# Pooling four batches of keys and values with accumulating transfers instead of VectorE reductions, and a new order for all engines

## The chip, the cores and the metric

The kernel runs on one core of a Trainium2 chip. The metric is the device time of one execution in microseconds, the median of several runs. Before the change it is 791.49 us (three runs, 791.37 to 791.86).

## The reference

Attention of 8 batches with 8 heads of 64 on 576 tokens, with keys and values averaged over groups of 8 neighbours (72 keys are left), and behind it a normalisation, a two-layer network (512 to 2048 to 512, relu) and a residual:

```python
k_p = k.reshape(B, H, Sp, pool, D).mean(axis=3)        # pool = 8, Sp = 72
v_p = v.reshape(B, H, Sp, pool, D).mean(axis=3)
scores = scale * np.matmul(q, k_p.transpose(0, 1, 3, 2))
attn = softmax(scores); attn_out = np.matmul(attn, v_p)
x = attn_out.transpose(0, 2, 1, 3).reshape(B, S, H * D)
xn = (x - mu) / np.sqrt(var + 1e-06) * g_ln
return x + np.maximum(xn @ w_ch1, 0.0) @ w_ch2
```

All is float32. The kernel makes each float32 factor from a high and a low float16 part and a product from three matmuls.

## The kernel before, in words

The 4608 tokens are 36 tiles of 128, four tiles to a chunk of 512 columns, nine chunks. Each tile goes through `stage_a` (load q, scores, softmax numerators; the maximum `mx` at L800, the difference `e` at L805), `probs_turned`, and `stage_b`, that is `values` (its product with the pooled values is scaled to the tile `x` at L950 on VectorE, then measured for the normalisation) and `parts_turned` (transposes of x on TensorE, L881). Chunks 0 and 1 take the network directly (`ffn_in` with matmuls at L1116 and results in `ring` at L1125 on ScalarE and L1127 on VectorE, `ffn_out` with sums at L1330); later chunks take a seven-product scheme (`product` at L1160, `out_seven` at L1277, sums at L1294). Its factors are made between them: ScalarE casts (L1196), VectorE and GpSimd subtract (L1198, L1215 to L1219); `sums_w2` makes sums of w2 with temporaries in the tile `kr` (L1239 on VectorE, L1244 to L1252 on GpSimd). At the start `convert` rebuilds the weights (L527 to L543), and `split_w` cuts them into parts, the high one on ScalarE (L483), the low one on VectorE (L490).

Keys and values must be pooled for each batch before its tiles. `half_k` and `half_v` do half a batch each: a load on SP's queue per pair of heads (288 KB into `kr`, L645) or per head (144 KB into `vr`, L659), and a reduction over 8 values: on VectorE with one `tensor_reduce` (L655 into `kblk`, L666 into `vp`), or for batch 2's keys and batch 1's and 2's values on GpSimd with three additions.

Nothing is ordered by a scheduler. Each stage is a generator, and two lists of tokens, `START` and `STEADY`, say which generator goes on by one step next ("HV.4.0" is the next step of half_v(4, 0)). So every engine's queue stands in the order of the lists, and an engine waits at its next instruction even where a later one could run. `kr` and `vr` have two buffers each, and `kr` is shared with `sums_w2`.

Of the kernel before, what the change touches and what calls it, by code (L numbers as in the profile page):

```python
# [63 lines left out]
START = """
LN.2 Q.0 LK.0 LN.2 LK.1 R.1.0 Q.1 A.0 R.1.1 R.1.2 K0 V0 K0 A.0 R.1.3 A.0 A.0 K0 R.1.3 R.1.2 HV.1.0 LK.0 LK.1 LG V0 R.2.0
E.0.0 LG V0 C.1.0 C.1.0 C.1.0 C.1.0 R.2.0 E.0.0 E.0.0 V0 V0 E.0.1 A.1 A.1 V0 A.1 E.1.0 C.1.1 V0 Q.1 C.1.1 E.0.1 C.1.1
C.1.1 E.0.0 V0 V0 C.1.2 C.1.3 E.0.1 C.1.2 E.1.0 E.0.1 E.1.1 HV.1.0 E.1.1 HV.1.0 E.1.1 C.1.3 E.1.1 E.1.0 HV.1.0 E.1.0
R.2.1 HV.1.0 HK.1.0 R.2.1 A.2 A.2 M1.0 A.2 A.2 B.0 A.1 M1.0 M1.0 M1.0 S.1.0 E.2.0 B.0 S.1.0 C.2.0 S.1.1 C.1.2 R.1.1 B.0
E.2.1 Q.0 HV.1.0 S.1.0 A.3 E.2.1 E.2.0 A.3 A.3 C.1.3 S.1.1 HK.1.0 E.2.1 A.3 E.2.0 E.2.1 B.0 B.0 B.0 B.0 S.1.2 E.2.0
R.1.0 B.1 HK.1.0 R.2.2 E.3.0 B.1 R.2.2 E.3.1 E.3.0 E.3.1 E.3.0 E.3.1 B.1 B.1 B.1 B.1 B.1 C.1.3 E.3.1 E.3.0 HV.1.0 C.2.0  # L70
HK.1.0 C.1.2 S.1.2 B.2 B.2 HV.1.1 C.2.2 S.1.3 HV.1.1 C.2.1 B.2 HV.1.0 B.2 B.2 C.2.0 B.2 B.2 S.1.3 HK.1.0 C.2.0 S.1.3 B.3
HK.1.1 HK.1.1 S.1.2 HK.1.1 C.2.1 HK.1.1 HK.1.1 C.2.1 C.2.1 B.3 F.0.0.0 F.0.1.0 F.0.0.0 F.0.1.0 F.0.0.0 R.2.3 D.0 R.2.3
F.0.1.0 A.4 F.0.0.0 F.0.2.0 A.4 F.0.1.0 F.0.3.0 A.4 HV.1.0 HV.1.1 C.2.2 HV.1.1 B.3 C.2.3 F.0.2.0 F.0.3.0 F.0.2.0 A.4
F.0.2.0 A.4 F.0.3.0 F.0.3.0 C.2.3 D.0 F.0.4.0 R.1.4 HV.1.1 A.5 A.5 A.5 C.2.2 C.2.2 HV.1.1 HV.1.1 C.2.3 F.0.4.0 B.3 B.3
B.3 B.3 R.1.4 F.0.5.0 A.5 F.0.6.0 R.1.5 M2.0 M2.0 F.0.5.0 F.0.4.0 F.0.6.0 F.0.4.0 A.5 M2.0 M2.0 R.1.6 S.1.1 A.6 S.2.0
A.6 R.1.7 C.1.4 R.1.7 F.0.5.0 A.4 R.1.5 A.4 HV.1.1 F.0.5.0 F.0.6.0 A.6 S.2.0 F.0.7.0 F.0.0.1 HV.1.1 F.0.0.1 F.0.1.1
HV.1.1 HV.1.1 F.0.1.1 F.0.7.0 HV.1.1 F.0.7.0 HV.1.1 HV.1.1 D.1 D.1 S.2.1 F.0.1.1 C.1.4 F.0.0.1 S.2.1 C.1.7 F.0.2.1 S.2.0
A.7 A.7 R.1.6 C.1.5 F.0.3.1 F.0.3.1 F.0.3.1 C.2.3 F.0.2.1 S.2.2 S.2.2 S.2.2 F.0.2.1 F.0.3.1 HV.1.1 F.0.4.1 F.0.2.1
F.0.5.1 C.1.6 M1.1 F.0.4.1 F.0.5.1 F.0.4.1 F.0.5.1 F.0.5.1 C.1.4 A.6 F.0.4.1 F.0.6.1 B.4 A.5 S.2.3 M1.1 B.4 M1.1 F.0.7.0
A.6 C.1.5 S.2.3 F.0.7.1 F.0.7.1 F.0.7.1 F.0.7.1 G.0.0.0 B.4 F.0.0.1 F.0.1.1 F.0.6.1 S.2.3 C.1.4 A.7 F.0.6.1 C.1.5 A.6  # L80
A.6 S.1.4 G.0.0.0 R.2.4 R.2.4 R.2.5 R.2.5 A.7 C.1.7 B.5 B.4 G.0.1.0 F.0.6.1 A.7 A.7 A.7 B.4 G.0.2.0 C.1.6 C.1.7 C.1.6
S.1.4 R.2.6 R.2.7 S.1.5 B.5 B.5 S.1.5 G.0.1.0 R.2.6 R.2.7 G.0.2.0 G.0.2.0 HK.2.0 G.0.3.0 C.2.4 S.1.6 C.2.5 S.1.6 B.6 B.4
C.2.4 G.0.1.0 B.4 S.1.7 G.0.3.0 S.1.7 F.0.8 HV.2.0 G.0.3.0 B.5 C.2.4 B.5 B.5 F.0.8 B.6 F.0.8 F.0.9 C.2.5 B.5 C.2.6
F.0.10 A.5 C.2.7 C.2.6 F.0.8 F.0.9 F.0.9 F.0.6.0 F.0.11 C.2.5 C.2.7 C.2.5 C.2.6 C.2.7 C.2.7 HK.2.0 F.0.10 C.2.6 F.0.11
B.6 C.2.4 C.1.5 M2.1 S.1.4 F.0.9 HK.2.0 F.0.12 M1.1 HK.2.1 F.0.10 A.8 HK.2.1 HK.2.0 HV.2.0 F.0.10 S.1.7 M2.1 M2.1 S.2.4
S.1.5 F.0.11 HV.2.0 F.0.12 S.2.4 F.0.12 A.8 S.2.5 F.0.12 F.0.13 S.2.4 F.0.11 S.2.5 S.2.5 HK.2.0 HV.2.0 HV.2.0 F.0.13 B.6
F.0.14 HV.2.0 C.1.7 HK.2.1 B.7 HV.2.0 G.0.0.0 S.2.6 F.0.14 HK.2.1 F.0.15 B.6 HK.2.1 F.0.13 F.0.13 S.2.6 S.2.7 S.2.7
F.0.14 F.0.14 F.0.15 S.2.7 HV.2.0 F.0.15 C.1.6 B.7 A.8 B.7 F.0.15 HV.2.0 B.7 A.8 HK.3.0 G.0.0.1 HV.2.1 HK.3.0 HV.2.1 B.7
A.8 HV.2.1 HV.2.1 HV.2.1 B.6 A.8 A.9 G.0.1.1 G.0.2.1 S.1.6 HV.2.1 B.6 B.7 HV.2.1 HV.3.0 G.0.0.1 G.0.1.1 A.9 G.0.2.1 B.7
A.8 A.9 A.9 G.0.3.1 A.9 T.1.0 HV.2.1 A.10 A.10 A.11 A.9 G.0.3.1 T.1.0 G.0.3.1 G.0.3.1 HV.2.1 F.1.0 A.9 B.8 T.1.0 T.1.0  # L90
F.1.0 HK.3.0 A.10 G.0.1.1 G.0.1.1 F.1.1 T.1.0 A.11 B.8 T.1.0 F.1.0 HV.2.1 S.2.6 T.1.0 S.2.1 T.1.0 F.1.2 F.1.0 T.1.0 A.10
T.1.0 HV.2.1 F.1.1 T.1.0 T.1.0 HV.2.1 F.1.1 F.1.2 F.1.2 F.1.3 HV.2.1 F.1.4 F.1.2 F.1.5 HV.2.1 HV.3.0 HV.3.0 T.1.1 HV.2.1
HV.2.1 G.0.2.1 F.1.1 F.1.4 F.1.4 G.0.2.1 HV.3.0 F.1.4 F.1.3 HV.3.0 A.10 A.11 A.10 HV.3.0 F.1.3 T.1.1 A.11 HV.3.0 F.1.3
F.1.6 B.9 F.1.6 T.1.1 F.1.5 HV.3.0 HV.3.0 A.10 T.1.1 A.11 HV.3.1 F.1.5 T.1.1 G.0.0.1 F.1.7 T.1.1 A.11 G.0.0.1 F.1.6
F.1.5 HV.3.1 T.1.1 A.11 HV.3.1 T.1.1 F.1.7 F.1.7 G.1.0.0 G.1.0.0 G.1.0.0 B.9 HV.3.1 G.1.1.0 HV.3.1 F.1.6 T.1.1 HV.3.1
G.1.2.0 HV.3.1 T.1.1 T.1.1 M2.1 HK.3.1 T.1.1 T.0.0 T.0.0 T.0.0 T.0.0 HV.3.1 T.0.0 T.0.0 V.10 G.1.3.0 T.0.0 T.0.0 HK.3.0
HK.3.0 T.0.0 T.0.0 F.1.7 T.0.0 G.1.2.0 HV.3.1 T.0.0 F.1.8 T.0.1 G.1.1.0 F.1.9 T.0.1 F.1.8 T.0.1 G.1.3.0 G.1.3.0 T.0.1
V.10 B.8 B.8 T.0.1 T.0.1 T.0.1 T.0.1 F.1.10 HV.3.1 F.1.8 HV.3.1 F.1.8 HV.3.1 T.0.1 F.1.9 U.0.1 U.0.0 F.1.11 F.1.10
F.1.11 F.1.9 T.0.1 F.1.9 B.8 F.1.10 B.11 B.8 F.1.10 U.0.1 G.1.1.0 F.1.12 B.11 U.0.1 T.0.1 F.1.13 F.1.12 T.0.1 F.1.13
F.1.11 F.1.11 F.1.14 F.1.12 F.1.14 F.1.13 F.1.13 B.9 F.1.15 F.1.15 B.9 U.1.1 B.9 U.1.0 F.1.14 F.1.14 F.1.15 F.1.15 B.9  # L100
B.9 V.10 V.10 HV.3.1 V.10 U.1.0 G.1.0.1 V.10 G.1.1.1 HV.3.1 F.1.12 U.1.0 HK.3.1 HK.3.1 V.10 V.10 G.1.2.1 G.1.0.1 X X
B.11 B.11 B.11 B.11 G.1.1.1 G.1.2.0 G.1.3.1 HV.3.1 HV.3.1 B.11 G.1.0.1 B.11 G.1.0.1 B.11 U.0.0 U.0.0 HK.3.1 HK.3.1 U.1.1
U.1.1 G.1.2.1 G.1.2.1 G.1.2.1 G.1.1.1 G.1.1.1 G.1.3.1 G.1.3.1 G.1.3.1
# [1358 lines left out]
```

## Time and profile before

| | |
|---|---|
| median of three runs | 791.49 us |
| the profiled execution | 792.71 us, of which the span of the trace is 791.0 us |
| TensorE (PE) busy | 772.5 us of the span (98%) |
| VectorE (DVE), GpSimd (POOL), ScalarE (ACT) busy | 628.3, 492.3, 469.5 us |
| mean granted TensorE clock | 1.00 of full speed |
| share of the 16 DMA engines in use by the main queue | 65.1% |

The profiled execution is one execution with the profiler on; 1.7 us of its time lie around the span. PE is the engine that is nearly always busy, so the end moves with what PE waits for. Busy time of the other engines costs nothing by itself; it counts where PE, or an engine that PE waits for, stands still for it.

### The profile page before, as it was taken

Reading aid. Unit: us, or ns where it says so; the run is one execution under the profiler, and the core shown is the slowest. Engines: PE = TensorE matmul, PEld = TensorE weight load, DVE = VectorE, ACT = ScalarE, POOL = GpSimd, SP = SyncE. Lnnn points to the kernel's source line nnn. Section 1 sums busy time; section 2 is a strip of 40 time slices with the busy share of each in tenths; the row PEclk is TensorE's granted clock in tenths of the full one; section 3 lists DMA queues with packets and bytes.
Section 4 is the critical chain, followed back from the end, with each engine's and each line's share of the span. In section 5 each row is a group of like instructions: output and inputs, shape, how many; then the busy total and the mean of one; then the engine's idle time right before and its main releaser. Section 6 shows DMA issues by size and latency. Waiting matters only on the chain. (4 is left out here: it accounts for less than half of the span.)

```text
span 791.0 us, 18982 instructions
## 1 busy us (share of the span) xinstructions
PE 772.5 (98%) x7458; PEld 592.8 (75%) x7458; DVE 628.3 (79%) x1296; ACT 469.5 (59%) x880; POOL 492.3 (62%) x597
## 2 busy tenths in 40 slices
...
GB/s 353 302 247 180 252 137 80 170 106 78 43 128 177 151 167 225 186 258 190 204 202 164 241 169 255 151 205 180 228 93 208 176 179 141 175 144 150 81 120 134
DMA packets 181513, 139.01 MB, mean 176 GB/s; under 512 B 143792, under 2 KB 151600, under 8 KB 179248
## 3 DMA queue, kind: packets, MB, share of 16 engines
q1 hardware_dynamic: 180272, 136.91, 65.1%
...
q10 hardware_dynamic: 1152, 0.90, 0.5%
...
## 5 line engine op out<-in xcount | busy, mean ns | idle before, releaser
L1277 PE MATMUL ps_f<-ring,w 128*128 128x256 f16 x2016 | 231.7, 273 | 1.5 <-DVE x L1294 1.0
L1277 PEld LDWEIGHTS <-w 128*128 128x128 f16 x2016 | 196.2, 98 | 25.8 <-issue 1.8
L1160 PE MATMUL ps_f<-zts,w 128*128 128x256 f16 x1680 | 208.1, 273 | 1.3 <-DVE x L1330 0.8
L1160 PEld LDWEIGHTS <-w 128*128 128x128 f16 x1680 | 162.7, 98 | 22.6 <-issue 2.1
L1319 PE MATMUL ps_f<-w,ring 128*128 128x512 f16 x576 | 126.6, 379 | 0.1
L1319 PEld LDWEIGHTS <-ring 128*128 128x128 f16 x576 | 56.0, 98 | 66.2 <-DVE ring L1127 0.9
L1179 ACT COPY raw<-ps_f 128x256 f32<-128x256 f32 x160 | 56.2, 372 | 81.7 <-PE ps_f L1160 69.3
L1160 PE MATMUL ps_f<-zts,tsp 128*128 128x256 f16 x672 | 92.1, 273 | 0.5 <-DVE raw L1174 0.3
L1116 PE MATMUL ps_f<-zts,w 128*128 128x512 f16 (+1 forms) x480 | 86.5, 336 | 2.9 <-DVE ring L1127 1.6
L1196 ACT CAST w<-w 128x512 f16<-128x512 f32 x96 | 59.0, 619 | 42.3 <-POOL w L1219 24.2
L1116 PEld LDWEIGHTS <-w 128*128 128x128 f16 x480 | 45.8, 98 | 38.8 <-issue 2.7
L1198 POOL TENSOR_TENSOR w<-w 128x512 f16<-128x512 f32 x48 | 57.4, 1197 | 25.5 <-ACT w L1196 22.9
L1160 PEld LDWEIGHTS <-tsp 128*128 128x128 f16 x672 | 64.5, 98 | 8.8 <-issue 0.7
L1215 POOL TENSOR_TENSOR w<-raw 128x256 f32<-128x256 f32 x32 | 25.9, 809 | 64.9 <-ACT raw L1207 42.9
L1294 DVE SCALAR_TENSOR_TENSOR x<-ps_f,y,x 128x256 f32<-128x256 f32 (+1 forms) x84 | 42.6, 518 | 28.5 <-PE ps_f L1277 27.5
L826 POOL TENSOR_TENSOR phl<-e,phl 128x512 f16<-128x512 f32 x32 | 41.1, 1285 | 37.5 <-ACT phl L816 28.9
L1085 POOL TENSOR_TENSOR hl<-raw,hl 128x640 f16<-128x640 f32 x28 | 42.4, 1517 | 17.0 <-ACT hl L1083 16.8
L1294 DVE SCALAR_TENSOR_TENSOR x<-ps_f,cy,x 128x256 f32<-128x256 f32 (+1 forms) x84 | 42.1, 516 | 12.1 <-PE ps_f L1277 11.3
L1198 DVE TENSOR_TENSOR w<-w 128x512 f16<-128x512 f32 x48 | 38.5, 803 | 8.9 <-ACT w L1196 8.9
L1198 DVE TENSOR_TENSOR w<-raw,w 128x512 f16<-128x512 f32 (+1 forms) x64 | 41.6, 654 | 3.3 <-ACT w L1196 3.1
L1179 ACT COPY phl<-ps_f 128x256 f32<-128x256 f32 x64 | 23.1, 372 | 31.9 <-PE ps_f L1160 29.2
L1174 DVE TENSOR_TENSOR raw<-ps_f,raw 128x256 f32<-128x256 f32 x80 | 32.9, 415 | 11.0 <-PE ps_f L1160 7.4
...
## 6 DMA issues: line engine op xcount, KB each, us to landing
...
```

The lines of the kernel that those rows point to most:

```text
L826: nc.gpsimd.tensor_tensor(out=ph[:, 0, :, KA:P], in0=e[:, :, 0:KA], in1=ph[:, 0, :, 0:KA], op=ALU.subtract)
L1085: nc.gpsimd.tensor_tensor(out=zhl[:, 1, :], in0=src, in1=zhl[:, 0, :], op=ALU.subtract)
L1116: nc.tensor.matmul(ps, lhsT=w[:, part, fs], rhs=zT[:, kz, cols], start=(n == 0), stop=(n == 3 * NKT - 1),)
L1160: nc.tensor.matmul(ps, lhsT=w[:, part, f * P : (f + 1) * P], rhs=z, start=m in (1, 2, 4, 5) and n == 0, stop=m in (2, 3, 4, 7) and n == 3 ...
L1174: nc.vector.tensor_tensor(out=o, in0=ps, in1=o, op=ALU.add)
L1179: nc.scalar.copy(out=o, in_=ps)
L1196: nc.scalar.copy(out=hi, in_=src)
L1198: engine.tensor_tensor(out=lo, in0=src, in1=hi, op=ALU.subtract)
L1215: nc.gpsimd.tensor_tensor(out=s_tmp[:, 0], in0=r01, in1=r11, op=ALU.add)
L1277: nc.tensor.matmul(ps, lhsT=wt[2][:, left, part, f * HC + u * P : f * HC + (u + 1) * P], rhs=b[:, f // FPB, wp, f % FPB], start=n < 4 and ...
L1294: nc.vector.scalar_tensor_tensor(out=x, in0=ps, scalar=scale, in1=x, op0=ALU.mult, op1=ALU.add)
L1319: nc.tensor.matmul(ps, lhsT=h[:, part, i, cols], rhs=w[:, wp, j], start=(n == 0), stop=(n == 3 * NFT // 2 - 1),)
```

## The change

For batches 4 to 7 (`BY_DMA`) the eight values of a group are added by transfers. Keys: all four pairs of a batch are laid out so that the eight neighbours are cut into four parts of two. One tile [128 x 576] takes the first part with a plain load on SP's queue, and three loads issued by GpSimd add the other parts onto it in SBUF, each after the one before has landed; one VectorE reduction then adds the two values that are left, for all four pairs at once (128x288 out of 128x576). Values: the same for four heads at a time (72x256 out of 72x512), so two chains a batch. The bytes read from HBM stay the same. In all 48 plain loads (16 of 288 KB, 32 of 144 KB) become 12 plain and 36 adding loads of the same sizes, and the 48 reductions of these batches become 12. Batches 0 to 3 are pooled as before.

Both token lists are written anew. But for the steps that pool batches 4 to 7 they hold the same tokens as often as before, in another order. The core of the diff (of the lists the lines in which batch 4's first steps stand):

```diff
+BY_DMA = (4, 5, 6, 7)
...
-P.2.0.0.6 P.2.0.0.6 HV.4.0 KW.1.1 KW.1.1 A.12 A.12 P.2.0.1.6 TW.0.0.0 TW.0.0.0 TS.2 TW.0.0.0 TW.0.0.0 P.2.0.1.6
+P.2.0.0.6 P.2.0.0.6 HV.4.0 KW.1.1 KW.1.1 A.12 A.12 P.2.0.1.6 TW.0.0.0 TW.0.0.0 TS.2 TW.0.0.0 TW.0.0.1 TW.0.0.0 TW.0.0.1
...
+    def added(tile, parts):
+        nc.sync.dma_start(out=tile, in_=parts[:, 0])
+        for j in range(1, POOL // 2):
+            yield
+            nc.gpsimd.dma_start(out=tile, in_=parts[:, j], accum_op=ALU.add)
+
     def half_k(b, i):
+        if b in BY_DMA:
+            if i == 0:
+                kraw[b, 0] = kr = wk2.tile([P, KV, POOL], F32, name="kr")
+                parts = kT[b].rearrange("p a k l -> p (a k l)").rearrange("p (j m) -> p j m", j=POOL // 2)
+                yield from added(kr.rearrange("p k l -> p (k l)"), parts)
+                return
+            kr = kraw.pop((b, 0)).rearrange("p k l -> p (k l)").rearrange("p (l c) -> p c l", l=2)
+            nc.vector.tensor_reduce(
+                out=kblk[b % NKB].rearrange("p a k -> p (a k)"), in_=kr, axis=AX.X, op=ALU.add
+            )
+            return
         yield from prep_k(b, (2 * i, 2 * i + 1))

     def half_v(b, i):
+        if b in BY_DMA:
+            if i == 0:
+                vp[b] = wk1.tile([KV, H, D], F32, name="vp")
+            vr = wk2.tile([KV, D, POOL], F32, name="vr")
+            parts = v[b].rearrange("p h d l -> p (h d l)").rearrange("p (i j m) -> p i j m", i=2, j=POOL // 2)
+            yield from added(vr.rearrange("p d l -> p (d l)"), parts[:, i])
+            yield
+            vr = vr.rearrange("p d l -> p (d l)").rearrange("p (l c) -> p c l", l=2)
+            nc.vector.tensor_reduce(
+                out=vp[b][:, 4 * i : 4 * i + 4].rearrange("p h d -> p (h d)"), in_=vr, axis=AX.X, op=ALU.add
+            )
...
```

The diff takes a line out above these functions, so a line of before stands one lower there (L1127 becomes L1126); the adding load is L1373 of the changed kernel.

In the order of VectorE, the first place is in START, where the second tile's attention output is scaled: rows 47 to 52 are `convert`'s join (L543), a reduction of keys, `split_w`'s low part (L490), and the three steps of `values` that end in x (L950). Before:

```order
47 L543 SCALAR_TENSOR_TENSOR w_91<-w_91,raw 128x1024
48 L655 TENSOR_REDUCE kblk_114<-kr 128x72
49 L490 SCALAR_TENSOR_TENSOR w_90<-w_90,gs 128x1024
50 L940 TENSOR_SCALAR sm<-ps_a,cv 128x8
51 L948 RECIPROCAL rs<-sm 128x8
52 L950 TENSOR_TENSOR x<-ps_a,rs 128x512
```

And now:

```order
46 L654 TENSOR_REDUCE kblk_114<-kr 128x72 x2
47 L489 SCALAR_TENSOR_TENSOR w_90<-w_90,gs 128x1024
48 L939 TENSOR_SCALAR sm<-ps_a,cv 128x8
49 L947 RECIPROCAL rs<-sm 128x8
50 L949 TENSOR_TENSOR x<-ps_a,rs 128x512
51 L959 BN_STATS st<-x 128x6
52 L960 BN_AGGR ln<-st 128x2
53 L542 SCALAR_TENSOR_TENSOR w_91<-w_91,raw 128x1024
54 L654 TENSOR_REDUCE kblk_114<-kr 128x72
```

The join of weights with `raw` (L543, now L542) has moved from ahead of x to behind it, and one more reduction of keys stands ahead.

The second place is VectorE a little further in START, where the first `ring` tiles of chunk 0 are taken out of PSUM between the softmax steps `mx` and `e` of a later tile, the maximum and scale of a batch's values (`mv` to `cv`), and maxima of weights (`wm`). Before:

```order
82 L1127 SCALAR_TENSOR_TENSOR ring<-ps_f,ring 128x256 x2
83 L800 TENSOR_REDUCE mx<-ps_a 128x8
84 L805 TENSOR_TENSOR e<-ps_a,mx 128x576
85 L675 TENSOR_REDUCE mv<-vp 72x1
86 L438 TENSOR_SCALAR rowmax<-mv 72x1
87 L439 TENSOR_SCALAR rowmax<-rowmax 72x1
88 L478 TENSOR_REDUCE allmax<-ps_m 128x1
89 L445 TENSOR_SCALAR sv<-allmax 128x1
90 L742 TENSOR_SCALAR cv<-sv 128x1
91 L743 TENSOR_SCALAR cv<-sv 128x1
92 L744 TENSOR_SCALAR cv<-allmax 128x1
93 L1127 SCALAR_TENSOR_TENSOR ring<-ps_f,ring 128x256
```

And now:

```order
85 L526 TENSOR_REDUCE wm_101<-raw 128x1
86 L1126 SCALAR_TENSOR_TENSOR ring<-ps_f,ring 128x256
87 L477 TENSOR_REDUCE allmax<-ps_m 128x1
88 L444 TENSOR_SCALAR sv<-allmax 128x1
89 L741 TENSOR_SCALAR cv<-sv 128x1
90 L742 TENSOR_SCALAR cv<-sv 128x1
91 L743 TENSOR_SCALAR cv<-allmax 128x1
92 L1126 SCALAR_TENSOR_TENSOR ring<-ps_f,ring 128x256 x2
93 L489 SCALAR_TENSOR_TENSOR vb<-vp,sv,vh 72x8x64
94 L799 TENSOR_REDUCE mx<-ps_a 128x8
95 L804 TENSOR_TENSOR e<-ps_a,mx 128x576
```

The steps `mx` and `e`, which stood ahead of the third ring tile (row 93 of before), now stand behind the third and the fourth (row 92).

The third place is GpSimd's queue in STEADY, with the last steps of one `sums_w2` (L1252, L1244 to L1248), low parts of z (L1085) and of the softmax numerators (L826, L829). Before:

```order
194 L1085 TENSOR_TENSOR hl<-z,hl 128x512
195 L1252 TENSOR_TENSOR phl_116<-kr,phl_116 128x4x128
196 L968 COPY ln<-cv 128x2
197 L1085 TENSOR_TENSOR hl<-z,hl 128x512
198 L826 TENSOR_TENSOR phl_115<-e,phl_115 128x8x64
199 L829 TENSOR_TENSOR phl_115<-e,phl_115 128x8x8
200 L1244 TENSOR_TENSOR kr<-kr 128x128
201 L1245 TENSOR_TENSOR kr<-kr 128x128
```

And now, with the three adding loads of batch 4's keys (L1373):

```order
199 L1373 DMA kr<-in_kT_dram 128x576
200 L1251 TENSOR_TENSOR phl_116<-kr,phl_116 128x4x128
201 L1084 TENSOR_TENSOR hl<-z,hl 128x512 x2
202 L1373 DMA kr<-in_kT_dram 128x576
203 L967 COPY ln<-cv 128x2
204 L825 TENSOR_TENSOR phl_115<-e,phl_115 128x8x64
205 L828 TENSOR_TENSOR phl_115<-e,phl_115 128x8x8
206 L1373 DMA kr<-in_kT_dram 128x576
207 L1243 TENSOR_TENSOR kr<-kr 128x128
208 L1244 TENSOR_TENSOR kr<-kr 128x128
```

Between the second and the third adding load stand a copy, L825 and L828 only; the third has to wait for the second to land, and the steps of `sums_w2` stand behind it.

## Rows read from the trace of the kernel before

**Rows 1.** The page, part 1: busy time, share, instructions of each engine.

```profile
PE 772.5 (98%) x7458; PEld 592.8 (75%) x7458; DVE 628.3 (79%) x1296; ACT 469.5 (59%) x880; POOL 492.3 (62%) x597
```

**Rows 2.** Waits of PE over the span: total us, times, longest.

```profile
PE ps_m L723 <- DMA w<-in_kvn_dram: 6.8, 1, 6.8
PE ps_f L1116 <- DVE ring L1127: 1.6, 3, 1.2
PE ps_m L881 <- DVE x L950: 1.0, 1, 1.0
...
PE ps_f L1116 <- DVE w L490: 0.7, 1, 0.7
...
PE ps_f L1116 <- ACT w L483: 0.5, 1, 0.5
```

**Rows 3.** Windows: busy of each engine, PEclk, DMA share, GB/s.

```profile
40.00:80.00 40.00, 36.46 (x432) 27.80 (x429) 36.49 (x73) 37.66 (x57) 30.61 (x37) 1.00 0.74 213
...
240.00:771.80 531.80, 529.20 (x5521) 450.47 (x5520) 429.80 (x930) 332.33 (x678) 340.85 (x418) 1.00 0.70 179
240.00:300.00 60.00, 59.36 (x588) 41.39 (x587) 56.43 (x125) 34.18 (x71) 41.02 (x58) 1.00 0.74 174
300.00:360.00 60.00, 60.00 (x581) 45.46 (x579) 52.99 (x111) 38.04 (x75) 48.88 (x67) 1.00 0.90 221
```

**Rows 4.** The lines of the two pooling reductions: min/median/max ns.

```profile
L655 DVE TENSOR_REDUCE kblk<-kr x24: 721/743/747, 35.5 to 585.4; 128x72 f32<-128x576 f32 x24
...
L666 DVE TENSOR_REDUCE vp<-vr x40: 649/672/683, 156.7 to 517.4; 72x64 f32<-72x512 f32 x40
```

**Rows 5.** Timeline of DVE, 38 to 45: start, us, line, operation.

```profile
38.16 1.98 DVE L543 SCALAR_TENSOR_TENSOR w<-w,raw 128x1024 int32<-128x1024 int32 x1
...
40.73 2.63 DVE L490 SCALAR_TENSOR_TENSOR w<-w,gs 128x1024 f16<-128x1024 f32 x1
...
43.77 0.69 DVE L950 TENSOR_TENSOR x<-ps_a,rs 128x512 f32<-128x512 f32 x1
```

**Rows 6.** Timeline of DVE, 62 to 73, idle before in brackets.

```profile
63.29 0.76 DVE L805 TENSOR_TENSOR e<-ps_a,mx 128x576 f32<-128x576 f32 x1
...
66.17 0.41 DVE L1127 SCALAR_TENSOR_TENSOR ring<-ps_f,ring 128x256 f16<-128x256 f32 x1
...
71.35 0.76 DVE L1127 SCALAR_TENSOR_TENSOR ring<-ps_f,ring 128x256 f16<-128x256 f32 x2 [0.90 <-ACT ring L1125]
```

**Rows 7.** Timeline of DVE, 98 to 103.

```profile
100.53 0.75 DVE L1330 SCALAR_TENSOR_TENSOR x<-ps_f,cy,x 128x512 f32<-128x512 f32 x1
101.32 1.28 DVE L490 SCALAR_TENSOR_TENSOR w<-w,gs 128x1024 f16<-128x1024 f32 x1
```

**Rows 8.** Groups of POOL, 240 to 720: busy us, mean ns, idle before.

```profile
L826 POOL TENSOR_TENSOR phl<-e,phl 128x512 f16<-128x512 f32 x24 | 29.6, 1235 | 28.6 <-ACT phl L816 20.0 <-DVE phl L1174 8.7
...
L968 POOL COPY ln<-cv 128x2 f32<-128x2 f32 x21 | 6.5, 311 | 0.0
```

**Rows 9.** Issues of the pooling loads on SP: min/median/max ns.

```profile
L645 SPq DMA_DIRECT2D kr<-in_kT_dram x28: 332/425/1413, 25.9 to 563.9; - x28
...
L659 SPq DMA_DIRECT2D vr<-in_v_dram x56: 299/358/962, 9.2 to 511.6; - x56
```

**Rows 10.** Timeline of SP and of POOL: one load and its reader; the last store.

```profile
17.21 0.40 SPq L659 DMA_DIRECT2D vr<-in_v_dram  x1
...
23.81 0.73 POOL L669 TENSOR_TENSOR vr<-vr 72x256 f32<-72x256 f32 x1 [0.54 <-DMA vr<-in_v_dram]
...
788.24 0.33 SPq L1305 DMA_DIRECT2D out_dram<-x  x1
```

**Rows 11.** Timeline of POOL, one copy at two places.

```profile
31.20 1.18 POOL L968 COPY ln<-cv 128x2 f32<-128x2 f32 x1
...
46.95 0.18 POOL L968 COPY ln<-cv 128x2 f32<-128x2 f32 x1
```

**Rows 12.** Waits of ACT, 240 to 791: total us, times, longest.

```profile
ACT w L1196 <- POOL w L1219: 24.2, 12, 4.2
```

More of the change, by code (lines that the diff above doesn't have):

```diff
@@ L69 @@
[L69 to L73, printed above, removed]
@@ L104 @@
+F.1.14 F.1.14 F.1.15 F.1.15 V.10 G.1.0.1 V.10 HV.3.1 V.10 G.1.1.1 U.1.0 V.10 HV.3.1 F.1.12 U.1.0 HK.3.1 HK.3.1 V.10 V.10
+G.1.0.1 X X B.11 B.11 G.1.2.1 B.11 B.11 G.1.1.1 G.1.3.1 HV.3.1 HV.3.1 B.11 G.1.0.1 B.11 G.1.0.1 B.11 U.0.0 U.0.0 HK.3.1
+HK.3.1 U.1.1 U.1.1 G.1.2.1 G.1.2.1 G.1.2.1 G.1.1.1 G.1.1.1 G.1.3.1 G.1.3.1 G.1.3.1
 """
@@ new lines @@
+Z.26.1 XT.26.1 EL.5.1.3 Z.26.1 EP.5.1.1.0 XT.26.1 LW.5.1.3 A.28 EL.5.1.1 P.5.1.3.3 P.5.1.2.7 ER.5.1.2 EP.5.1.1.1
+O.5.1.0.0 P.5.1.3.4 P.5.1.3.4 O.5.1.0.0 EL.5.1.2 P.5.1.3.7 O.5.1.0.0 P.5.1.3.7 ER.5.1.2 O.5.1.1.0 O.5.1.1.0 O.5.1.1.0
+B.27 B.27 B.27 ER.5.1.2 O.5.1.0.1 LW.5.1.4 LW.5.1.4 A.29 A.29 ES.5.1.2 EP.5.1.2.0 O.5.1.1.1 EP.5.1.2.0 EP.5.1.2.0
+P.5.1.3.2 EP.5.1.1.1 EP.5.1.1.1 ER.5.1.3 ER.5.1.3 O.5.1.0.1 ER.5.1.3 LW.5.1.5 LW.5.1.5 O.5.1.1.1 ES.5.1.2 ES.5.1.3
+ES.5.1.2 Z.27.0 Z.27.1 Z.27.1 EP.5.1.3.0 Z.27.0 O.5.1.1.1 EP.5.1.3.0 O.5.1.2.0 O.5.1.2.1 A.30 O.5.1.3.0 O.5.1.3.1
```

601 lines of the change are left out of this document (302 added, 299 removed).

## The prediction, made before the changed kernel ran

> **What bounds the kernel now.** I began with the busy shares: PE is busy 772.5 of 791.0 us [rows 1], so a change can pay only in PE's 18.5 idle us or by taking work off PE, and this one takes none off. The second view is PE's own waits [rows 2]: 6.8 us at the start for the first load; the rest are waits for VectorE and ScalarE of 1.2 us at most. None names GpSimd, and after the start none names a transfer. The third view is a table of windows [rows 3]: from 240 us, where batch 4's pooling begins, to 771.8, where PE's last run of matmuls starts, PE idles 531.80 - 529.20 = 2.6 us, and from 300 to 360 not at all, though VectorE is busy 52.99 of these 60 us. So VectorE, however full, has no debt to PE where the reductions stand. The granted clock is 1.00 in each row. The stretch from 40 to 80 us is the opposite: PE lacks 3.5 us there, and VectorE is as busy as PE (36.49 against 36.46). There only the order is changed, not the pooling.
>
> **The change part by part.**
>
> *The reductions.* The 16 of keys and 32 of values cost VectorE 16 x 0.743 + 32 x 0.672 = 33.4 us [rows 4]. The 12 that replace them read the same number of values per instruction (576 or 512 a partition), so I price them alike: 4 x 0.743 + 8 x 0.672 = 8.3 us. VectorE is relieved of 25.1 us between 240 and 585 us. Most it could be worth is the 2.6 us that PE waits there; least is nothing, and I take nothing: it is work that PE's queue hides already, and the waits left are for sums and splits that stand in line for PE's own results.
>
> *The loads on SP.* 36 issues leave SP, at 0.36 to 0.43 us each [rows 9]: no engine waits for SP's time, so nothing.
>
> *The adding loads on GpSimd.* The trace of before has no transfer issued by GpSimd, so both costs are bounds. The issue holds GpSimd 0.36 us (the median of values on SP) at least, and 1.41 (the longest on SP) at most, plus what contention with VectorE adds. That contention is seen: one copy of 128x2 takes 0.18 us alone and 1.18 beside VectorE's two-input instructions [rows 11], so 1.0 more, 2.4 in all. I take 1.0 us, a third of the way up, nearer to the rows on SP: 36 us over 36. For the time to land, the last store has 791.0 - 788.24 - 0.33 = 2.4 us from its issue to the end of the span, and a load of 144 KB in the crowded start took 23.81 - 17.21 = 6.6 us until its reader began [rows 10]. I take about 3, nearer to the first, since these loads are small.
>
> The cover is GpSimd's own idle time. From 300 to 360 us, its fullest stretch, it is busy 48.88, idle 11.1 [rows 3]. Counting its queue by the places of the same steps, eight of the 36 adding loads fall there: 8 us at 1.0 each, covered. From 240 to 300 it has 19.0 idle for ten. Each adding load but the first of a chain waits for the one before to land, and GpSimd's queue stands behind it. Most pairs have 3.5 us of work or more between them; the tightest, the second and third load of batch 4's keys (the third place shown), has a copy, an L826 and an L829: 0.31 + 1.24 + about 0.4 = 1.9 us [rows 8]. At 3 us to land GpSimd stands 1.1 us there, at 6.6 it stands 4.7; behind it are sums of w2, which PE uses much later. Nothing for PE at the value taken.
>
> The Trainium skill, "DMA: Bandwidth & Descriptors", section "Anatomy of one DMA — SWDGE (gpsimd) path", fits a transfer issued by GpSimd as 2.0 us plus its bytes at 436 GB/s; my estimate from that is 2.7 us for 288 KB and 2.3 for 144, and the sum by it would be the same. No run of before shows it.
>
> *The transfer engines.* Reading the destination back adds work to the same 16 engines. In the fullest stretch their share is 0.90 at 221 GB/s, 13.3 MB [rows 3]; the eight adding loads there are about 1.5 MB (192 KB on average), 12% of it. If they took twice the time, the share would come to 1.0: full, but hardly over. PE waits for no transfer there now, so nothing, with the upper case below.
>
> *The order of START.* Here the change touches PE's waits. First place: x at 43.77 is waited for 1.0 us by L881 [rows 2], and VectorE came without a pause through a join of weights of 1.98 us [rows 5]. The join now stands behind x, one more reduction of 0.74 ahead: x is 1.24 us earlier and the wait goes. Second place: L1116 waits 1.2 us of its 1.6 for the ring tile of 66.17 [rows 2, 6]; `mx` and `e`, 0.75 and 0.76 us, no longer stand ahead of it. I count 1.3 of the 1.6 us as gone. PE would so reach 72 us about 2.3 us sooner. But at 100 to 103 us it waits again, 0.7 for the low parts of VectorE and 0.5 for the high parts of ScalarE [rows 2], and VectorE ran almost without a pause before: the low part L490 that frees PE comes straight behind an L1330 of 0.75 us [rows 7]. What PE gains before can last only as far as VectorE itself comes sooner here. Up to that low part its queue now holds one L1330 (0.75 us) less; the rest of its work is the same. Besides, it can lose pauses such as the 0.90 at 71.35 [rows 6], which waits for ScalarE. I take 0.75 of pauses: 0.75 + 0.75 = 1.5 us. Bounds: nothing, if new pauses appear; 2.3, if all that PE gains is kept. None of the waits of [rows 2] lies behind 103 us, and the 2.6 us of STEADY are short ones, so what is gained stays.
>
> *The end.* The last rows of all queues are the same: nothing.
>
> Sum, against the profiled execution: 792.71 - 1.5 = 791.2; its span 791.0 - 1.5 = 789.5. The profiled execution is 1.22 us above the median, so for the median 791.49 - 1.5 = **790.0 us**. A measurement of this kernel can tell about 0.2%, 1.6 us, from no change.
>
> **The rivals.**
>
> *Faster: the new lists also clear the waits of STEADY.* With 25 us less on VectorE, and all steps placed anew, most of the 2.6 us could go, and the whole 2.3 of START stay: 791.49 - 2.3 - 2.6 = 786.6 at the extreme, about 788 with a little over a half of each kept. For it: none of these waits is forced by PE's own chain alone. Against it: every list that is written anew can make as many small waits as it removes.
>
> *Slower: GpSimd is held by its own loads.* Place: 300 to 360 us. Point from which it decides: 11.1 / 8 = 1.4 us for each adding load, waits for landing in it. At 2.4 us GpSimd comes 8 x 2.4 - 11.1 = 8.1 us late. ScalarE's casts L1196 wait for GpSimd's L1219 up to 4.2 us now [rows 12] without a wait of PE, so of 8.1 us I count 4.2 as absorbed; 3.9 reach PE: 791.49 - 1.5 + 3.9 = 793.9. For it: PE's second factors come from this chain (L1219, L1196, L1198, L1277). Against it: PE waits for GpSimd nowhere now.
>
> The Trainium skill, "SBUF — State Buffer", section "Who interferes with whom", speaks for this rival: VectorE and GpSimd share a pair of ports, and a VectorE instruction that takes the pair for itself starves GpSimd's writing of descriptors. The copy of 0.18 and 1.18 us agrees that a two-input instruction of VectorE blocks GpSimd's reads; that it delays issues, no run here shows. The same section says that a `tensor_reduce` never contends, by which the removed reductions give GpSimd nothing back.
>
> *No change: START's gain is lost at 103 us.* VectorE's pauses move instead of going, and one L1330 less is made up by one wait more: 791.5, between 791 and 792.
>
> **How the numbers follow.** My forecast (788.9 to 791.0 as its own range) has a chance of 0.42, and about half of that lies more than 0.2% below 791.49, under 789.9. Faster rival 0.22, slower rival 0.22, no change 0.14. That gives faster 0.43, same 0.35, slower 0.22. The range goes from 787.4, inside the faster rival, to 794.4, half a microsecond over the slower rival's price; outside are some 0.05 below and 0.1 above.
>
> **What would show it.** Right: PE's wait for x at L881 gone or under 0.3 us, its waits for the ring under 0.8 in sum, PE at its place of 103 us sooner by about 1.5 us; VectorE busy about 603 us in place of 628; adding loads on GpSimd near 1 us each, and still no wait of PE for GpSimd. Wrong: ScalarE's waits for GpSimd at L1196 doubled with PE waiting behind them at L1160 or L1277; PE waiting for a transfer between 240 and 600 us; or PE's waits around 100 us as long as before, or new ones between 103 and 240 us.

## The result, and the profile after

The changed kernel is slower: 797.87 us in the median of six runs (796.03 to 801.58) against 791.78 (791.37 to 792.15) of the kernel before in the same batch of runs; ratio 1.0082, 95% interval 1.0060 to 1.0103. The forecast was 790.0 us in a range up to 794.4, so it was wrong, and on the wrong side. The runs also lie seven times as far apart as those of before, 5.6 us against 0.8. The profiled execution is the fastest of the six (796.03 us, span 794.2), so its trace shows less of the loss than the median has.

The busy shares of the page, to be held against [rows 1]:

```profile
PE 772.6 (97%) x7458; PEld 592.5 (75%) x7458; DVE 612.7 (77%) x1260; ACT 469.7 (59%) x880; POOL 516.8 (65%) x633
```

PE does the same work and stands idle 21.6 us instead of 18.5. VectorE is relieved by 15.6 us, not by 25.1. Where the idle time sits, the windows tell (columns as in [rows 3]; the first row is of the kernel before, the others are of the changed one):

```profile
360.00:420.00 60.00, 60.00 (x661) 53.35 (x659) 52.13 (x112) 39.78 (x83) 35.05 (x43) 1.00 0.80 192
...
40.00:80.00 40.00, 37.92 (x456) 29.22 (x455) 36.80 (x78) 39.17 (x60) 31.26 (x38) 1.00 0.84 239
80.00:120.00 40.00, 40.00 (x256) 19.23 (x256) 34.73 (x60) 32.21 (x42) 25.99 (x29) 1.00 0.73 184
240.00:300.00 60.00, 57.24 (x541) 39.33 (x539) 51.01 (x113) 33.30 (x66) 41.99 (x63) 1.00 0.87 175
300.00:360.00 60.00, 58.66 (x568) 44.11 (x566) 50.85 (x99) 36.30 (x74) 52.29 (x72) 1.00 0.89 212
360.00:420.00 60.00, 56.98 (x616) 49.81 (x614) 45.21 (x100) 35.82 (x75) 38.68 (x47) 1.00 0.90 186
```

The stretch of START is better than before: 37.92 of 40 us from 40 to 80 (it was 36.46), and 40.00 of 40 after that. In the three windows from 240 to 420 us PE loses 2.8, 1.3 and 3.0 us, 7.1 in all; before it lost 0.6, nothing and nothing ([rows 3] and the first row here). The transfer engines are busier for the same rate: a share of 0.87 for 175 GB/s from 240 to 300, where it was 0.74 for 174, and 0.90 for 186 from 360 to 420, where it was 0.80 for 192. The waits of PE (total us, times, longest) name what stands before 4.2 of the 7.1 us:

```profile
PE ps_m L722 <- DMA w<-in_kvn_dram: 6.5, 1, 6.5
PE ps_a L931 <- DMA pt<-phl: 4.2, 4, 1.6
PE ps_f L1159 <- DVE raw L1173: 0.9, 3, 0.5
...
PE ps_f L1115 <- DVE ring L1126: 0.2, 1, 0.2
```

The waits for the ring and for x, on which START's term rested, are gone (0.2 us are left of the first). New is the second row: PE waits 4.2 us for transfers `pt<-phl`. These are the transposes of the softmax numerators, which SP issues (`dma_start_transpose`, L836) once GpSimd has made their low parts. "PE waiting for a transfer between 240 and 600 us" is one of the signs by which the prediction was to be known as wrong. Of the adding loads the views show the time of an issue on GpSimd (min/median/max ns), their queue from 240 to 590 us (packets, MB, share of the 16 engines), and the median us from issue to landing (last figure):

```profile
L1373 POOL DMA_DIRECT2D vr<-in_v_dram x24: 807/832/1181, 226.8 to 512.9; - x24
L1373 POOL DMA_DIRECT2D kr<-in_kT_dram x12: 843/880/1210, 264.2 to 579.2; - x12
...
q0 software_dynamic: 3936, 6.93, 12.8%
...
kr<-in_kT_dram POOLq DMA_DIRECT2D x12, 288.0 KB, 6.2
vr<-in_v_dram POOLq DMA_DIRECT2D x23, 144.0 KB, 5.0
```

An issue takes 0.83 to 0.88 us, near the 1.0 that I had taken; landing takes 5.0 and 6.2 us in the median, not 3. 35 of the 36 adding loads lie in these 350 us; for 6.93 MB they take 12.8% of the 16 engines. GpSimd waits for landings, and ScalarE for GpSimd, as follows:

```profile
POOL kr L1373 <- DMA kr<-in_kT_dram: 4.3, 2, 2.4
POOL vr L1373 <- DMA vr<-in_v_dram: 4.0, 2, 2.2
...
ACT w L1195 <- POOL w L1218: 22.5, 11, 4.0
```

GpSimd stands 8.3 us at four places, but the casts of ScalarE that wait behind it wait no longer than before (24.2 us, longest 4.2, in [rows 12]).

How one of the transposes comes late, in the timelines of GpSimd, SP and PE (start, length, what):

```profile
397.76 0.88 POOL L1373 DMA_DIRECT2D kr<-in_kT_dram  x1
398.35 1.18 POOL L1373 DMA_DIRECT2D vr<-in_v_dram  x1
...
397.85 2.15 SPq L836 DMA_TRANSPOSE pt<-phl  x1
...
407.10 0.20 PE L931 MATMUL ps_a<-va,pt 128*128 128x65 f16 x1 [1.41 <-DMA pt<-phl]
```

Two adding loads, 288 and 144 KB, go out just as the transpose does. PE comes to it 7.8 us after its issue, waits 1.41, and starts 9.25 us after it. The same tile before, in the timelines of SP and PE:

```profile
393.07 2.06 SPq L837 DMA_TRANSPOSE pt<-phl  x1
...
402.99 0.19 PE L932 MATMUL ps_a<-va,pt 128*128 128x65 f16 x1
```

There PE comes 9.9 us after the issue and does not wait. At the other three waits, too, an adding load goes out within 0.4 us of the transpose. PE came 5.2, 5.8 and 9.4 us after the issue and had to wait until 5.7, 7.4 and 10.1 us after it; before, it came 5.5, 7.1 and 9.5 us after the issue of the same tiles' transposes and did not wait. So two things have changed. The transposes have less time in the changed kernel, by 0.2 to 2.1 us at all four places; had PE come as late after the issue as before, 1.1 of the 4.2 us would be left. And at these three they land later than they did before, by 0.2 to 0.6 us at least. For the fourth see run 5, which has the new list without adding loads. What the transfer engines do in the same stretch is seen in two strips of the DMA view, from 397 to 409 us, 0.3 us a figure (busy tenths, then GB/s). Before:

```profile
DMA  9679786421020000337988100000009999999995
GB/s 375 181 136 215 242 265 260 179 106 48 14 55 0 0 0 0 61 82 239 280 300 341 62 0 0 0 0 0 0 11 207 215 206 215 217 219 207 218 226 108
```

And after:

```profile
DMA  8710000897899999999799989997999999630000
GB/s 330 277 69 8 0 0 22 166 170 71 94 108 113 194 165 166 146 211 151 69 121 67 84 48 111 75 72 24 276 213 239 280 362 410 266 109 7 7 7 20
```

After, from 399 to 405 us, the engines are nearly full at 24 to 211 GB/s, about 110 in the median; before, full engines moved over 200 (at the strip's end), and nothing moved from 400.6 to 401.8 us, so the transpose issued at 393.07 had most likely landed by 7.5 us after its issue.

### The profile page after: what moved, and what is told of

The parts are those of the page before. It is cut to its first block, busy times and chain, and to the rows that moved or that the text cites. A ratio compares the mean times of both kernels' runs of the same rounds, so it can differ in the third digit from the quotient of the medians.

```text
span 794.2 us, 18940 instructions
## 1 busy us (share of the span) xinstructions
PE 772.6 (97%) x7458; PEld 592.5 (75%) x7458; DVE 612.7 (77%) x1260; ACT 469.7 (59%) x880; POOL 516.8 (65%) x633
## 4 chain that ended last, share of the span: by engine, by line
PE 71%; DVE 8%; ACT 7%; POOL 6%; DMA 4%; issue 2%; POOLq 0%; SPq 0%; DVEq 0%; ACTq 0%
PE ps_f L1159 25%; PE ps_f L1276 21%; PE ps_f L1318 12%; PE ps_f L1115 8%; DMA pt<-phl 2%; DVE w L1197 2%; PE ps_a L789 2%; DMA zts<-hl 1%; DVE x L1293 1%; ACT w L482 1%; PE ps_a L931 1%; PE ps_a L932 1%; DVE kr L1238 1%; PE ps_m L722 1%; ACT w L534 1%
## 5 line engine op out<-in xcount | busy, mean ns | idle before, releaser
L1159 PE MATMUL ps_f<-zts,w 128*128 128x256 f16 x1680 | 208.4, 273 | 2.2 <-DVE x L1329 0.8
L1159 PEld LDWEIGHTS <-w 128*128 128x128 f16 x1680 | 162.6, 98 | 23.7 <-issue 3.0
L1159 PE MATMUL ps_f<-zts,tsp 128*128 128x256 f16 x672 | 91.7, 273 | 0.5 <-DVE raw L1173 0.5
L1197 POOL TENSOR_TENSOR w<-w 128x512 f16<-128x512 f32 x48 | 59.3, 1235 | 28.3 <-ACT w L1195 22.1
L1159 PEld LDWEIGHTS <-tsp 128*128 128x128 f16 x672 | 64.7, 98 | 9.0 <-issue 0.7
L825 POOL TENSOR_TENSOR phl<-e,phl 128x512 f16<-128x512 f32 x32 | 41.7, 1304 | 38.0 <-ACT phl L815 37.8
L1214 POOL TENSOR_TENSOR w<-raw 128x256 f32<-128x256 f32 x32 | 26.1, 814 | 54.4 <-ACT raw L1206 44.7
L1197 DVE TENSOR_TENSOR w<-w 128x512 f16<-128x512 f32 x48 | 40.3, 840 | 9.2 <-ACT w L1195 9.1
L1197 DVE TENSOR_TENSOR w<-raw,w 128x512 f16<-128x512 f32 (+1 forms) x64 | 43.6, 686 | 1.2 <-ACT w L1195 1.2
```

Source lines behind the costliest of these rows:

```text
L825: nc.gpsimd.tensor_tensor(out=ph[:, 0, :, KA:P], in0=e[:, :, 0:KA], in1=ph[:, 0, :, 0:KA], op=ALU.subtract)
L1159: nc.tensor.matmul(ps, lhsT=w[:, part, f * P : (f + 1) * P], rhs=z, start=m in (1, 2, 4, 5) and n == 0, stop=m in (2, 3, 4, 7) and n == 3 ...
L1197: engine.tensor_tensor(out=lo, in0=src, in1=hi, op=ALU.subtract)
L1214: nc.gpsimd.tensor_tensor(out=s_tmp[:, 0], in0=r01, in1=r11, op=ALU.add)
```

## The experiments

Three theories stood at the start. T1: adding is slow work for the transfer engines, and the transposes behind it land late. T2: the new STEADY list is too tight of itself. T3: GpSimd is held by its issues and landings, and what waits for GpSimd is late. Runs 2 and 4 to 11, but for run 10, leave out or overwrite a part of the sums for batches 4 to 7; they serve for their times and traces. Ratios are against the kernel before on the same chip; its medians there were 791.49 to 791.83 us.

**1. The new START alone.** The kernel before, with only `START` replaced.

```diff
-START = """ ... (before)
+START = """ ... (changed kernel)
```

> The kernel before with the changed START list alone: no adding transfers, the old STEADY list. The trace after shows PE about 2 us further at 240 us than before. If that gain is real and lasts to the end, the time is about 789.7 us (789.0 to 790.4). If the old STEADY gives it back, or the gain was one execution's chance, 791.8 us.

788.74 us (788.56 to 789.14), ratio 0.9963 (0.9951 to 0.9975). START's gain is real, it is 2.75 us, and the old STEADY keeps it. By 120 us PE has 2.3 us more of its work behind it than before (first row: before), and in the windows from 240 us on it is as busy as before:

```profile
0.00:120.00 120.00, 108.38 (x1042) 69.53 (x1043) 99.80 (x184) 95.67 (x131) 74.19 (x91) 1.00 0.77 244
...
0.00:120.00 120.00, 110.67 (x1054) 71.10 (x1055) 99.70 (x186) 97.24 (x134) 75.84 (x93) 1.00 0.81 246
...
240.00:300.00 60.00, 59.30 (x552) 40.32 (x549) 56.39 (x126) 34.18 (x68) 39.47 (x58) 1.00 0.77 180
300.00:360.00 60.00, 60.00 (x591) 46.58 (x591) 53.70 (x107) 35.70 (x73) 50.51 (x70) 1.00 0.89 220
360.00:420.00 60.00, 60.00 (x686) 53.09 (x684) 52.24 (x112) 41.73 (x87) 35.31 (x41) 1.00 0.77 185
```

Of the kernels with all of the computation in them, this is the fastest of the study, faster than before and after.

**2. Loads that overwrite.** The same 36 loads, waits and bytes, without adding.

```diff
-            nc.gpsimd.dma_start(out=tile, in_=parts[:, j], accum_op=ALU.add)
+            nc.gpsimd.dma_start(out=tile, in_=parts[:, j])
```

> The changed kernel with the 36 loads still issued by GpSimd at the same places with the same waits and bytes, but overwriting instead of adding (so the pooled keys and values of batches 4 to 7 are not the reference's). Theory T1 (adding is slow work for the transfer engines, and the transposes of the probabilities land late behind it): loads land in about 3 us, PE's waits at L931 for transposes fall from 4.2 us to under 1, time 789.5 to 792. Theory T2 (the new STEADY list stands too tight): 796 to 799 as now, with the same waits. Theory T3 (GpSimd is held by issuing and by waiting for landings): issues stay near 0.85 us, so most of the loss stays, 794 to 798. If it is any load issued by GpSimd, adding or not, that delays the transposes: 796 to 799.

795.11 us (793.17 to 798.89), ratio 1.0048 (1.0030 to 1.0066): 2.8 us better, but not what T1 alone asks for. The transfers, from 240 to 590 us:

```profile
q0 software_dynamic: 2432, 6.93, 7.8%
...
kr<-in_kT_dram POOLq DMA_DIRECT2D x12, 288.0 KB, 4.0
vr<-in_v_dram POOLq DMA_DIRECT2D x23, 144.0 KB, 3.8
```

For the same bytes they take 7.8% of the engines, not 12.8, and land in about 4 us; the waits for transposes fall to 0.7 us in all. An issue takes 0.54 to 0.57 us. Something else holds PE: its waits at L1159 for VectorE's sums have grown from 0.9 to 2.4 us.

**3. The new lists with VectorE's reductions.** The steps of batches 4 to 7 do a plain load and a reduction each, one load in flight per half, since the lists give them only five steps. Of the values (the keys are alike):

```diff
...
+            load_v(b, 4 * i)
+            for h in range(4 * i, 4 * i + 4):
+                yield
+                pool_v(b, h)
+                if h < 4 * i + 3:
+                    load_v(b, h + 1)
...
```

> The changed kernel's START and STEADY lists, but the steps of batches 4 to 7 do plain loads on SP and VectorE reductions, as before the change (one load in flight per half). T1: no adding transfers, so no late transposes: 789 to 791.5 us. T2 (list too tight): L931 waits for transposes as in the changed kernel, 795 us or more. T3: GpSimd is free of issues, 789 to 791.5.

799.56 us (799.06 to 803.90), ratio 1.0110 (1.0093 to 1.0127). Taken by itself this speaks for T2. But the run has a fault of its own: with one load in flight SP's queue stands at the next load until VectorE has read the last one,

```profile
SPq L658 <- DVE vp L665: 20.5, 10, 4.7
```

and all transfers that SP issues are queued behind, the transposes too (PE's waits for these are 0.6 us). How much of the 8 us comes from this was not measured, so it tells nothing sure of the lists, and I took run 5 in its place.

**4. An eighth of the columns.** Each adding load brings 64 columns.

```diff
+            nc.gpsimd.dma_start(out=tile[:, :64], in_=parts[:, j, :64], accum_op=ALU.add)
```

> The changed kernel with each adding load cut to 64 of its 576 or 512 columns (the pooled values are not the reference's): as many issues on GpSimd, as many waits, an eighth of the bytes added. T1: waits at L931 mostly gone, 789.5 to 792 us. T2: as now, 796 to 799. T3: issues of about 0.85 us stay, only landings get shorter, 793 to 797.

794.13 us (791.34 to 797.09, twelve runs), ratio 1.0030 (1.0017 to 1.0044), with no wait for a transpose among PE's longer ones. 3.7 us of the loss go with the bytes added; the rest is still there with an eighth of them. The trace is of the fastest of the twelve. Their mean granted clocks fall in two groups: 1.000 in the four fastest (791.3 to 792.1 us), 0.997 to 0.999 in the other eight (794.0 to 797.1); what TensorE's clock does is seen in run 10.

**5. No adding loads.** The 36 loads are left out.

```diff
-            nc.gpsimd.dma_start(out=tile, in_=parts[:, j], accum_op=ALU.add)
```

> The changed kernel, both its lists, with the 36 adding loads left out (each chain has its first plain load and the last reduction, so three quarters of the values of batches 4 to 7 are missing). T2 (the new STEADY list itself is too tight): 794 us or more. T1 and T3 (the adding loads do it, by their bytes or by what they do on GpSimd): about 788 to 789.5, as START's gain alone gave, and VectorE's instructions stretched beside GpSimd go back from 21 to 25 us of excess to about 13.

789.84 us (788.17 to 791.48), ratio 0.9974 (0.9965 to 0.9983). The new STEADY list, with 48 reductions cut to 12, is about where the old one is (run 1, interval up to 0.9975): T2 falls as a cause of the loss by itself. The tile of above, in the timelines of SP and PE:

```profile
395.31 1.85 SPq L836 DMA_TRANSPOSE pt<-phl  x1
...
402.99 0.19 PE L931 MATMUL ps_a<-va,pt 128*128 128x65 f16 x1
```

PE comes 7.7 us after the issue, as in the changed kernel, and the transpose is there; with adding loads it takes 9.25. So at this tile the new list leaves 2.2 us less than the old, and only the adding loads make a wait of it. The relief of VectorE is not priced alone here, since list and relief change together; together they gain nothing that can be told.

**6. Tiny adding loads.** 16 partitions by 64 columns, 4 KB.

```diff
+            nc.gpsimd.dma_start(out=tile[:16, :64], in_=parts[:16, j, :64], accum_op=ALU.add)
```

> The changed kernel with each adding load cut to 16 partitions by 64 columns (sums not the reference's): the same 36 issues and waits on GpSimd, next to no bytes, an eighth of the rows. If the loss is bytes on the transfer engines: 789 us. If it is that GpSimd's issue and what follows it hold VectorE's two-input instructions (stretched by 2 to 3 us where a GpSimd issue stands near): issues of 0.8 us stay and so does the loss that the run with an eighth of the columns showed, 793 to 795; if the time of an issue goes with its rows, issues fall under 0.5 us and the time to 790 or 791.

793.64 us (791.67 to 795.50), ratio 1.0024 (1.0014 to 1.0034): 3.8 us over run 5 with next to no bytes. An issue still takes 0.76 us, whatever it moves. PE's waits at L1159 for VectorE's sums are 4.6 us here, the longest 1.92. The timelines of GpSimd, VectorE and PE at that one:

```profile
370.85 0.73 POOL L1214 TENSOR_TENSOR w<-phl 128x256 f32<-128x256 f32 x1 [0.65 <-ACT phl L1206]
371.65 0.72 POOL L1215 TENSOR_TENSOR w<-w,phl 128x256 f32<-128x256 f32 x1
372.32 0.77 POOL L1373 DMA_DIRECT2D vr<-in_v_dram  x1
372.86 0.42 POOL L967 COPY ln<-cv 128x2 f32<-128x2 f32 x1
373.00 0.96 POOL L1217 TENSOR_TENSOR w<-phl,w 128x256 f32<-128x256 f32 x1
373.69 0.94 POOL L1218 TENSOR_TENSOR w<-phl 128x256 f32<-128x256 f32 x1
374.38 1.61 POOL L1084 TENSOR_TENSOR hl<-raw,hl 128x640 f16<-128x640 f32 x1
...
372.70 3.57 DVE L1197 TENSOR_TENSOR w<-phl,w 128x256 f16<-128x256 f32 x1
376.20 1.40 DVE L1173 TENSOR_TENSOR raw<-ps_f,raw 128x256 f32<-128x256 f32 x4
...
376.99 1.25 PE L1159 MATMUL ps_f<-zts,tsp 128*128 128x256 f16 x10 [1.92 <-DVE raw L1173]
```

VectorE's subtraction of 128x256, which takes 0.4 us elsewhere, takes 3.57. It ends at 376.27, 0.28 us after GpSimd's last instruction of the row ends (374.38 + 1.61). From the issue on, each GpSimd instruction begins before the one ahead of it has ended (372.32 + 0.77 is 373.09, the next begins at 372.86), so there is no gap; the pair L1214 and L1215 ahead of the issue, where one waits for the other, has a gap of 0.07. That made a fourth theory, L: VectorE's subtraction reads two tiles of SBUF, GpSimd's instructions read SBUF too, and VectorE's stays out until GpSimd's stream has a gap. Over 240 to 600 us I summed, for VectorE's instructions that stand alone in a row, what they take above the tenth percentile of their own kind, where that is over 0.3 us: 13 us before, 21 in the changed kernel, 24 here, 15 without the loads. The rival, G, is T3 again: it is GpSimd's own time that counts.

**7 and 8. The adding loads in the old STEADY.** New START, old STEADY, batches 4 to 7 by adding loads; once keys and values, once keys alone. In these two the old list starts the reduction of the keys ahead of the last additions, so the pooled keys lack a part.

> The new START list, the STEADY list of before, and batches 4 to 7 pooled by adding loads at the places where their loads stood in it. To be held against the new START with the old pooling, 788.74 us. T1 or T3 (the adding loads cost by themselves): 791 to 798. T2 (only the new list costs): 788 to 789.5.

> As the run before, but only the keys of batches 4 to 7 by adding loads (12 of 36 issues, half of the bytes), the values by plain loads and VectorE. If bytes decide, about half of that run's loss over 788.74; if the number of issues decides, a third; if neither costs in this list, 788 to 789.5.

848.84 us (847.59 to 850.12) and 803.10 (802.72 to 803.50), ratios 1.072 and 1.0142. The old list sets the steps of a chain close together, so GpSimd stands at landings, in run 7 for 42 us:

```profile
POOL vr L1375 <- DMA vr<-in_v_dram: 31.0, 10, 6.9
...
POOL kr L1375 <- DMA kr<-in_kT_dram: 11.0, 4, 4.7
```

Here GpSimd's queue is held by its own loads, as in the slower rival of the prediction, and PE waits for VectorE and ScalarE (10.2 and 10.1 us at L1161). A part of run 7's loss is TensorE's clock, 0.976 in the mean of the profiled execution. The new list does spread the loads as it must.

**9 and 10. Gaps.** Behind each issue three tiny instructions on GpSimd, each waiting for the one ahead, with tiny and with full adding loads.

```diff
             nc.gpsimd.dma_start(...)
+            nc.gpsimd.memset(gap, 0.0)
+            nc.gpsimd.tensor_copy(out=gap2, in_=gap)
+            nc.gpsimd.memset(gap2, 0.0)
```

> The run with tiny adding loads (793.64 us) with three tiny instructions on GpSimd behind each issue, each waiting for the one before, so that GpSimd's stream has gaps there (some 0.4 us more of GpSimd time each). Theory L (behind an issue GpSimd's instructions overlap without a gap and VectorE's two-input instructions are locked out until the first gap, 3.6 us in place of 0.4 at 372.7 us): VectorE's stretched instructions fall back to at most 1.2 us over their normal time, excess from 24 to about 15 us, PE's wait of 1.9 us at L1159 goes, time 790 to 792. Rival G (it is GpSimd's time that counts): GpSimd is 15 us busier, 794 to 796.

> The changed kernel itself (797.87 us) with the same three tiny instructions behind each issue. Theory L: 794 to 796, as the late landings of the transposes stay. Rival G: 798 to 800.

With tiny loads 791.34 us (790.40 to 792.92), ratio 0.9997 (0.9989 to 1.0006): 2.3 us better, with more work on GpSimd. The wait at L1159 and the busy shares:

```profile
PE ps_f L1159 <- DVE raw L1173: 0.6, 2, 0.4
...
PE 773.3 (98%) x7458; PEld 592.8 (75%) x7458; DVE 606.9 (77%) x1260; ACT 469.3 (59%) x880; POOL 529.5 (67%) x741
```

No instruction of VectorE is stretched by more than 1.2 us, the sum falls from 24 to 17 us. L holds, G falls. The 1.5 us that are left over run 5 have no cause shown. With full loads 798.65 us (796.12 to 801.74), ratio 1.0081: no gain. The stretching is gone there too (17 us), but PE's waits are for transposes:

```profile
PE ps_a L931 <- DMA pt<-phl: 4.3, 3, 1.9
PE ps_f L1159 <- DMA zts<-hl: 1.9, 2, 1.4
```

So the two causes don't add up. That VectorE's delay is hidden behind the late transposes would explain it, but no run shows it. The trace of run 10 shows a further cost of a late transpose. PE's longest wait for one, 1.92 us, ends at 268.73 us; the granted clock is 1.00 up to 268 us, and then:

```profile
268.00:272.00 4.00, 3.27 (x29) 1.76 (x30) 3.42 (x9) 3.26 (x5) 1.26 (x2) 0.76 1.14 249
272.00:276.00 4.00, 4.00 (x17) 1.67 (x16) 3.30 (x12) 1.85 (x3) 2.76 (x7) 0.81 0.96 140
```

From 276 us it is 1.00 again. By these two figures the clock stood for an estimated 3.4 of the 8 us at the lower of its levels, 1.2 GHz in place of 2.4, and PE is busy 774.9 us for the instructions that took it 772.6 in the changed kernel's trace. It does not follow on every such wait: behind the 1.92 us of run 6 the clock stayed at 1.00.

**11. Gaps, and loads that overwrite.**

```diff
+            nc.gpsimd.dma_start(out=tile, in_=parts[:, j])
```

> Gaps behind the issues, all bytes loaded by GpSimd's transfers, but overwriting instead of adding (sums not the reference's); between the tiny loads with gaps (791.34 us) and the adding loads with gaps (798.65). Theory A (adding is the slow work that delays the transposes): 791 to 792.5, no wait of PE for transposes over 1 us. Theory Q (any bytes on GpSimd's queue beside the transposes delay them): 796 us or more, with waits of PE at L931 or L1159 for transposes of 3 us or more in sum. Between 793 and 796: both.

792.15 us (789.78 to 793.52), ratio 1.0006 (0.9998 to 1.0015), 6.5 us under the adding loads with gaps. All the bytes go through GpSimd's queue here, and cost under 1 us over the tiny loads with gaps:

```profile
PE ps_a L931 <- DMA pt<-phl: 1.1, 1, 1.1
...
q0 software_dynamic: 2432, 6.93, 7.5%
```

It is the adding, not the bytes or the queue, that delays the transposes: theory A. The longer issue of an adding load (0.83 us for 0.54) is not it either, since run 9 has an issue nearly as long, and hardly any bytes, at 791.34 us.

**12. The old START.** The changed kernel with only `START` put back.

> The changed kernel with the START list of before: only that part undone. If START's 2.75 us and STEADY's loss add up: 797.87 + 2.75 = 800.6 us (798.5 to 802.5). If the later time of STEADY changes what collides: about 798.

800.30 us (796.74 to 803.87), ratio 1.0106 (1.0078 to 1.0135): 2.4 us over the changed kernel. That fits START's gain and STEADY's loss adding up, but the runs lie 7 us apart and the two intervals overlap, so the other forecast, about 798, isn't ruled out.

## Why the prediction was wrong

**The transfer engines: the step that failed.** I priced the second read of the destination by bytes, in the fullest window, and allowed twice the time. That size was not the fault: adding took the engines 12.8 for 7.8 of overwriting the same bytes, 1.6 times, and the share from 300 to 360 us came to 0.89, where it had been 0.90. What failed is the step from there to nothing, "PE waits for no transfer there now". That was true with unknown slack: the transposes of each tile stand between GpSimd's low parts and PE's next product, go through the same engines, and at the four places had 5.5 to 9.9 us. I never listed them, nor saw that the new list took up to 2.1 us of that away. Nor does the mean share of the fullest 60 us bear on it: all four waits stand outside that window, and at the one shown above what counted was a stretch of 6 us. The runs put a number on it: 798.65 against 792.15, 6.5 us, for adding instead of overwriting, with the gaps in both. Some of it is TensorE's lower clock behind the waits; the two traces have PE busy 774.9 and 773.0 us.

The Trainium skill, "DMA: Bandwidth & Descriptors", section "Issuing engines are not separate DMA queues", says that transfers of all issuing engines run on the same 16 engines and interleave. The late transposes agree; had I read it against SP's transposes and not only against the loads, the rival would have been there.

**The adding loads on GpSimd.** The issue was sized about right (0.83 to 0.88 for 1.0). The landing was taken from the wrong end of its bounds: 5.0 and 6.2 us, near the 6.6 of the crowded start, not 3. By the fit of the Trainium skill's "DMA: Bandwidth & Descriptors", section "Anatomy of one DMA — SWDGE (gpsimd) path", my estimate was 2.3 and 2.7; the measurement decides, and even the overwriting loads took 3.8 and 4.0. No wait of PE in the changed kernel's trace is put down to GpSimd's waits at landings, as predicted.

**The slower rival named the wrong path.** GpSimd did not become late for ScalarE. Its contention with VectorE, which I had from [rows 11] only as a slow GpSimd copy and only as a price of the issue, works the other way too: VectorE waits for GpSimd. It costs PE 2.3 us in the runs with tiny loads; what it costs with the full ones is not shown, since the gaps gained nothing there. The section "Who interferes with whom" of the Trainium skill's "SBUF — State Buffer" says that a VectorE instruction with two SBUF inputs contends with a GpSimd instruction that reads SBUF. The 3.57 us agree, and show that it can stay out over several instructions of GpSimd in a row.

**The reductions.** That their relief is worth nothing to PE fits run 5, but no run has it alone. VectorE's busy time fell by 15.6 and not 25.1 us, and 6.8 of the 15.6 come with the new START alone (621.5 us in run 1, with the same 1296 instructions). So 16 us are missing; 8 of them are the stretched instructions, 21 us against 13, the rest I can't place.

**START: the mechanism right, the term too small.** 1.5 us forecast, 2.75 measured in run 1 (2.4 by run 12, with its wide interval), over the upper bound of 2.3. I had let 100 to 103 us take back a part of PE's 2.3 us; PE has no wait at all from 80 to 120 us now, so it kept them, and a little more.

**The order of STEADY** I had as worth 0 to 2.6 us. Runs 1 and 5 tell no difference. What I did not look for is that it would leave the transposes less time.

By the runs the way from 791.5 to 797.9 is: less 2.75 for START, about 1 (not sure) for the new STEADY without adding loads, 3.8 for 36 issues on GpSimd with next to no bytes (2.3 of it VectorE locked out, 1.5 open), 4.2 for the full adding loads. Each is the difference of two runs that follow on each other, so that they add up is no test. What stays open is why the runs of one kernel lie several us apart with the new STEADY list (7 in run 12, 3 even without adding loads in run 5). The clock is a part of it where it fell, as in run 4, but all twelve of run 5 have 1.000; landings that vary (3.1 to 9.7 us) would explain another part, but were not tried apart from the rest.
